# The fourth row tile of the last layer: its accumulated sums turned by DMA transposes and laid into its PSUM bank by ScalarE

## The chip, the cores and the metric

The kernel runs on one core of one Trainium2 chip. The metric is the device time of one execution in microseconds (us). Engines are named as in the profile: PE (TensorE, the matrix engine), DVE (VectorE), ACT (ScalarE), POOL (GpSimd) and SP (SyncE, which issues most DMAs). PSUM is the memory that PE writes: 8 banks of 512 float32 columns on 128 partitions. SBUF is the on-chip memory that the other engines and the DMAs use.

## The reference

Six layers of a cross network over 4096 rows of 416 features, all in bfloat16:

```
B, F, D, L = 4096, 26, 16, 6          # Din = 26 * 16 = 416
x = x0
for l in range(6):
    x = x0 * (x @ ws[l] + bs[l]) + x
return x
```

## The kernel before

By induction every layer's result is x0 times a running sum: x after layer l is x0 * (1 + the sum over all layers so far of (x @ w + b)). So the kernel never restarts its PSUM accumulation: the banks hold the running sum S, each layer adds its product, and the next x is x0 * (S + a bias column). It works on the transposed matrix (features on partitions, rows along the columns).

The 4096 rows are cut into four blocks (`s` = 0 to 3) of 1024 rows, and a block into two halves (`h`) of 512. The 416 features are three chunks (`c`) of 128 and a tail of 32. `bank(h, c)` is 3h + c: banks 0 to 2 hold half 0, banks 3 to 5 half 1; banks 6 and 7 (`T_BANK`) hold the 32 tail features of both halves.

`Plan.add` records every operation with the data that it reads and writes, and works out its semaphore waits. Each engine then runs its own list strictly in the order written. Two engines never touch one bank at once: a reader of a bank also waits for the earlier readers of it on other engines (lines 39 and 40).

One layer of one block is, on PE: `main` for half 0 (36 matmuls), `tail_rows` (what the tail adds to the six banks, in two operations), `tail_outs` (the tail's own sums), `main` for half 1. DVE's `leave` (line 435) makes the next x from a bank, one per bank. ACT's `tail_halves` (line 445) takes the tail banks, POOL multiplies them by x0 (line 458), and ACT and POOL copy the swapped pieces (lines 422, 424).

After layer 5 the results of blocks 0 to 2 stand transposed. `transpose_block` turns them with DMA transposes on SP's queue (lines 475 and 480, SBUF to SBUF), and `store_block` lays the 32 tail features beside them (POOL, line 486) and stores the block (SP, line 492). The store of block s - 1 is issued in block s at layer 3, that of block 2 thus in the last block.

The last block's layer 5 is done otherwise (from line 605), so that no transposed result is left at the end. For each of eight row tiles `j` of 128 rows, x is the stationary operand and the weights stream, so the product comes out with rows on partitions:

- `row_main(j, start, narrow)`: three products (k = 0, 1, 2) into bank `ROW_BANKS[j]`. Narrow means that each is cut into four matmuls of 32 columns of the array.
- `row_sums(j, narrow)`: the running sum S up to layer 4 has to be added, and it stands transposed. Three matmuls of `sS_sb` against an identity matrix (again times four if narrow) turn it and add it to the bank in one step.
- `row_tails()`: what the tail features add, for all eight tiles at once.
- `finish(j, ...)`: times x0, by DVE (line 665), or by ACT (line 672) and POOL (line 676); then six stores (line 683).

The running sums are saved beforehand, in the step that the code calls `ending` (block 3, layer 4): `keep_sum(h, c, engine)` copies bank(h, c), with the bias column added, to `sS_sb` (ACT, line 467, five times; DVE, line 469, once). POOL makes `st_sb`, the same for the tail (lines 579 and 584). The order in the `ending` step is: on PE all of layer 4; on DVE six `leave` and one `keep_sum`; on ACT first the two `tail_halves`, then five `keep_sum` in the order (0,0), (0,1), (0,2), (1,0), (1,1). Of the last layer PE's order is:

```
for j in range(4):
    row_main(j, True, True)
for j in range(4):
    row_sums(j, True)
row_tails()
...
for j in range(4, 8):
    row_main(j, False, False)
    row_sums(j, False)
    finish(j, None)
```

All matmuls of the program carry line 287, that of a helper, so they are told apart by their tiles: `ps<-w_sb,xT_sb` is `row_main`, `ps<-ident,sS_sb` is `row_sums`, `ps<-wt_sb,xt_sb` and `ps<-ident,st_sb` are `row_tails`.

Of the kernel before, what the change touches and what calls it, by code (L numbers as in the profile page):

```python
# [8 lines left out]
ACTF = mybir.ActivationFunctionType  # L9
# [109 lines left out]
def bass_standalone__dcn_v2_cross__recsys_kernel(  # L119
# [6 lines left out]
    B, D = x0.shape  # L126
    L = ws.shape[0]
    NC = 3
    DF = 128 * NC
# [3 lines left out]
    NS = B // SB  # L133
    H = SB // 2
# [5 lines left out]
    CH = range(NC)  # L140

    with ExitStack() as es:

        def sb(name, shape, dt=BF16):
            return es.enter_context(nc.sbuf_tensor(name, shape, dt))
# [12 lines left out]
        t32_sb = sb("t32_sb", [128, 2, G], FP32)  # L158
        sS_sb = sb("sS_sb", [128, NC, SB])
        st_sb = sb("st_sb", [128, G])  # L160
        f32_sb = sb("f32_sb", [128, 2, D], FP32)
        xo_sb = sb("xo_sb", [128, NS - 1, NC, SB])
        xot_sb = sb("xot_sb", [128, NS - 1, G])
# [9 lines left out]
        ps = es.enter_context(nc.psum_tensor("ps", [128, 8, 512], FP32))  # L173
# [5 lines left out]
        P = Plan()  # L179
# [51 lines left out]
        for k in CH:  # L231
# [19 lines left out]
            writes=[("dummy",)],  # L251
# [12 lines left out]
                out=u_sb[:, :], in_=ones_sb[:, 0:L], pattern=[[1, L]],  # L264
                compare_op=ALU.is_ge, fill=0.0, base=1, channel_multiplier=-1,
            ), reads=[("ones",)], writes=[("u",)],
        )
        P.add("gpsimd", lambda e: e.memset(wc_sb[:, :, :], 0.0), writes=[("wc", "wt%d" % i) for i in range(3)])

        def replicate():  # L270
            for g, eng in ((1, "gpsimd"), (3, "scalar"), (2, "gpsimd")):
# [156 lines left out]
        def leave(s, l, h, c):  # L428
            if l == L - 1:
                dst, key = xo_sb[:, s, c, h * H:(h + 1) * H], ("xo", s, c, h)  # L430
            else:
                dst, key = xT_sb[:, (l + 1) % 2, c, h * H:(h + 1) * H], ("xT", (l + 1) % 2, c, h)
            o = s * SB + h * H
            P.add(
                "vector", lambda e: e.scalar_tensor_tensor(  # L435
                    out=dst, in0=ps[:, bank(h, c), :], scalar=cb_sb[:, c, l:l + 1], in1=x0T_sb[:, c, o:o + H],
                    op0=ALU.add, op1=ALU.mult,
                ), reads=[("ps", bank(h, c)), ("cb",), ("x0T", s, c, h)], writes=[key],
            )
# [24 lines left out]
        def keep_sum(h, c, eng):  # L464
            o, i, b = sS_sb[:, c, h * H:(h + 1) * H], ps[:, bank(h, c), :], cb_sb[:, c, L - 1:L]
            if eng == "scalar":
                fn = lambda e: e.activation(out=o, in_=i, func=ACTF.Identity, bias=b)  # L467
            else:
                fn = lambda e: e.tensor_scalar_add(o, i, b)
            P.add(eng, fn, reads=[("ps", bank(h, c)), ("cb",)], writes=[("sS", c, h)])  # L470

        def transpose_block(s):
            for c in CH:
                P.add(
                    "sync", lambda e, c=c: e.dma_start_transpose(
                        o_sb[:, s * JS:(s + 1) * JS, c * 128:(c + 1) * 128], xo_sb[:, s, c, :]
                    ), reads=[("xo", s, c, h) for h in HALVES], writes=[("o", s)], dma="oT%d" % s,
                )
            P.add(
                "sync", lambda e: e.dma_start_transpose(ot_sb[:, s, :, :], xot_sb[:, s, :]),  # L480
                reads=[("xot", s)], writes=[("ot", s)], dma="ot%d" % s,
            )
# [60 lines left out]
        for s in range(NS):  # L543
            for l in range(L):
                ending = s == NS - 1 and l == L - 2
                if s == NS - 1 and l == L - 1:
                    break
                if s == 0 and l == 0:
                    for k in CH:
                        for part in range(2) if k == 0 else (None,):  # L550
                            for m in CH:
                                main(s, l, 0, m, k, part)
                        if k == 1:
                            tail_in()
                            bias_sums()
                    tail_rows(s, l, True)
                    for c in CH:
                        leave(s, l, 0, c)
                    tail_outs(s, l, False)
                else:  # L560
                    for m in CH:
                        for k in CH:
                            main(s, l, 0, m, k)
                    tail_rows(s, l, l == 0)
                    for c in CH:
                        leave(s, l, 0, c)
                    tail_outs(s, l, False)
                if s == 0 and l == 1:
                    corner(2, L, "wt2")
                leave_tail(s, l, not ending)  # L570
                if l == 2 and 0 < s < NS - 1:
                    place_tail(s + 1)
                if s == 0 and l == 0:
                    corner(1, 2, "wt1")
                if l == 3 and s > 0:
                    store_block(s - 1)
                if ending:
                    P.add(
                        "gpsimd", lambda e: e.tensor_tensor(
                            out=bt_sb[:, :], in0=cb_sb[:, NC, L - 1:L], in1=cb_sb[:, NC, L - 2:L - 1], op=ALU.subtract  # L580
                        ), reads=[("cb",)], writes=[("bt",)],
                    )
                    P.add(
                        "gpsimd", lambda e, t=t32_sb[:, l % 2, :]: e.tensor_scalar_add(st_sb[:, :], t, bt_sb[:, :]),
                        reads=[("t32", l % 2), ("bt",)], writes=[("st",)],
                    )
                    for c in CH:
                        keep_sum(0, c, "scalar")
                for m in CH:
                    for k in CH:  # L590
                        main(s, l, 1, m, k)
                    leave(s, l, 1, m)
                if ending:
                    for c in CH:
                        keep_sum(1, c, ("scalar", "scalar", "vector")[c])
            if s < NS - 1:
                transpose_block(s)
            if s < NS - 2:
                load_transposed(s + 2, 0, SB)
                load_last_columns(s + 2)  # L600
            if s == NS - 2:
                load("sync", xr_sb[:, :, :], x0_v[:, (NS - 1) * JS:NJ, :], "xr", [("xr",)])


        s, l = NS - 1, L - 1
        ROW_BANKS = (6, 7, 0, 1, 2, 3, 4, 5)
        src, off = src_main(s, l)
        srct, tkey = src_tail(s, l)

# [7 lines left out]
        def row_main(j, start, narrow):  # L617
            b, h = ROW_BANKS[j], j // 4
            for k in CH:
                P.add(  # L620
                    "tensor", lambda pe, k=k: row_mm(
                        pe, ps[:, b, 0:D], src[:, k, off + j * 128:off + (j + 1) * 128], w_sb[:, l, k, :],
                        start and k == 0, narrow,
                    ), reads=[("w", l), src_key(s, l, k, h)], adds=[("ps", b)],
                )

        def row_sums(j, narrow):
            b, h = ROW_BANKS[j], j // 4

            def fn(pe):  # L630
                for c in CH:
                    ins = row_mm(
                        pe, ps[:, b, c * 128:(c + 1) * 128], sS_sb[:, c, j * 128:(j + 1) * 128], ident[:, :], False, narrow
                    )
                return ins

            P.add("tensor", fn, reads=[("ident",)] + [("sS", c, h) for c in CH], adds=[("ps", b)])

        def row_tails():
            for r in range(2):  # L640
                def fn(pe, r=r):
                    for g in range(4):
                        b = ROW_BANKS[2 * g + r]
                        mm(
                            pe, ps[:, b, 0:D], srct[quad(g), 0, r * 128:(r + 1) * 128], wt_sb[quad(g), l, :],
                            g >= 2, (32 * g, 0),
                        )
                    for g in range(4):
                        b = ROW_BANKS[2 * g + r]
                        ins = mm(  # L650
                            pe, ps[:, b, DF:D], st_sb[quad(g), r * 128:(r + 1) * 128], ident[quad(g), quad(g)],
                            False, (32 * g, 0),
                        )
                    return ins

                P.add(
                    "tensor", fn, reads=[("wt", wkey(l)), tkey, ("st",), ("ident",)],
                    adds=[("ps", ROW_BANKS[2 * g + r]) for g in range(4)],
                )
# [24 lines left out]
                reads=[("ol", j) for j in range(a, b)], writes=[("outl", a)], dma="outl%d" % a,  # L684
            )

        for j in range(4):
            row_main(j, True, True)
        for j in range(4):
            row_sums(j, True)  # L690
        row_tails()
        finish(0, None)
        finish(1, 0)
# [40 lines left out]
```

## Time and profile before

| what | value |
|---|---|
| runs | 128.41, 128.68, 128.70 us; median 128.68 us |
| the profiled execution | 128.06 us, of which its span (first to last instruction) is 126.6 us |
| PE busy | 123.0 us, 97% of the span, 2414 matmuls |
| DVE busy | 99.6 us, 79% |
| ACT busy | 43.6 us, 34% |
| POOL busy | 38.8 us, 31% |
| last layer of the last block | PE from 117.56 us to the end of its matmuls at about 123.9 us |
| last store | issued at 124.56 us, the last landing near the end of the span |
| store of block 2 | issued at 114.06 us; the three block stores take 4.4 us (median) from issue to landing |

The span is counted from the first instruction; all times below are from there. A group's duration is that of one instruction, but matmuls overlap in the array: 48 matmuls of 339 ns each are done in 2.28 us, so what a matmul costs PE is the distance to the next one. The chain of waits is the sequence of work that ended last, followed back from the end. "From issue to landing" of a DMA counts from the start of its issue on the queue's engine until its semaphore says that the data is there.

### The profile page before, as it was taken

What the parts mean: (1) busy time and instruction counts of PE and PEld (TensorE: products, weight loads), DVE (VectorE), ACT (ScalarE), POOL (GpSimd) and SP (SyncE); (2) the same over time, 40 slices, a digit from 0 to 9 for tenths busy, and PEclk for the clock granted to TensorE, in tenths of its full rate; (3) what the DMA queues carried; (4) which work ended last, traced back from release to release, by engine and by line L of the source; (5) the groups of instructions that cost most, each with busy time, mean ns of one, the idle gap of its engine ahead of it and who ended that gap; (6) DMA issues with size and microseconds to landing.
All of it is one profiled execution on the core that took longest, in us unless ns stands there. A gap on an engine that the chain in (4) does not pass through costs nothing.

```text
span 126.6 us, 5307 instructions
## 1 busy us (share of the span) xinstructions
PE 123.0 (97%) x2414; PEld 64.3 (51%) x2414; DVE 99.6 (79%) x156; ACT 43.6 (34%) x95; POOL 38.8 (31%) x81
## 2 busy tenths in 40 slices
PE   7999999999999999999999999999999999999991
PEld 5554554554555554545545545545545545555660
DVE  2467978879879779779779789788797797797873
ACT  2342523424205225225205224233223252253820
POOL 6505404314204124144014043152122241350450
PEclk9999999999999999999999999999999999999999
DMA  3998998100059791016037893108009480006117
GB/s 99 237 240 226 292 199 107 28 19 0 8 114 161 167 166 28 22 54 226 0 86 169 68 218 87 31 5 269 5 9 203 80 257 0 5 0 226 49 39 236
DMA packets 34934, 14.03 MB, mean 111 GB/s; under 512 B 25722, under 2 KB 34912, under 8 KB 34912
## 3 DMA queue, kind: packets, MB, share of 16 engines
q1 hardware_dynamic: 33744, 13.20, 47.3%
q10 hardware_dynamic: 1136, 0.49, 1.4%
q8 instruction: 19, 0.31, 1.0%
q14 instruction: 3, 0.02, 0.1%
q0 software_dynamic: 32, 0.01, 0.0%
HBM read 3.79 MB, written 3.41 MB: 57 GB/s over the span
## 4 chain that ended last, share of the span: by engine, by line
PE 97%; DVE 0%; issue 0%
PE ps L287 94%; PE ps L295 2%; PE ps L506 1%; DVE o_sb L665 0%
## 5 line engine op out<-in xcount | busy, mean ns | idle before, releaser
L435 DVE SCALAR_TENSOR_TENSOR xT_sb<-ps,cb_sb,x0T_sb 128x512 bf16<-128x512 f32 x120 | 80.9, 743 | 16.5 <-PE ps L287 16.5
L287 PE MATMUL ps<-xT_sb,w_sb 128*32 128x512 bf16 (+1 forms) x1596 | 84.2, 364 | 0.0
L287 PEld LDWEIGHTS ps<-xT_sb,w_sb 128*32 128x32 bf16 x1596 | 40.9, 97 | 37.2 <-issue 4.0
L445 ACT ACTIVATE t_sb<-ps,cb_sb 64x256 f32<-64x256 f32 x46 | 21.6, 469 | 57.2 <-PE ps L287 56.9
L458 POOL TENSOR_TENSOR xt_sb<-t_sb,x0t_sb 128x256 bf16<-128x256 f32 x20 | 13.4, 671 | 65.2 <-ACT t_sb L445 65.2
L422 ACT ACTIVATE xt_sb<-xt_sb 32x256 bf16<-32x256 bf16 x38 | 15.7, 414 | 15.1 <-POOL xt_sb L458 14.9
L287 PE MATMUL ps<-x0T_sb,w_sb 128*32 128x512 bf16 (+1 forms) x348 | 18.6, 358 | 0.1
L424 POOL COPY xt_sb<-xt_sb 32x256 bf16<-32x256 bf16 x38 | 14.9, 392 | 2.4
L435 DVE SCALAR_TENSOR_TENSOR xo_sb<-ps,cb_sb,x0T_sb 128x512 bf16<-128x512 f32 x18 | 12.1, 743 | 2.5 <-PE ps L287 2.5
L287 PEld LDWEIGHTS ps<-x0T_sb,w_sb 128*32 128x32 bf16 x348 | 8.8, 96 | 7.5 <-issue 0.8
L287 PE MATMUL ps<-xt_sb,wt_sb 32*128 32x512 bf16 (+1 forms) x152 | 11.6, 326 | 0.0
L287 PE MATMUL ps<-xt_sb,wc_sb 32*128 32x256 bf16 x76 | 7.3, 268 | 0.0
L287 PEld LDWEIGHTS ps<-xt_sb,wt_sb 32*128 32x128 bf16 x152 | 2.3, 91 | 8.1 <-DVE xT_sb L435 8.1
L458 POOL TENSOR_TENSOR xot_sb<-t_sb,x0t_sb 128x256 bf16<-128x256 f32 x3 | 2.0, 671 | 9.9 <-ACT t_sb L445 9.9
L287 PE MATMUL ps<-w_sb,xT_sb 128*32 128x416 bf16 (+1 forms) x60 | 5.1, 339 | 0.0
L665 DVE TENSOR_TENSOR o_sb<-ps,xr_sb 128x416 bf16<-128x416 f32 x6 | 3.4, 587 | 1.3 <-PE ps L287 1.0
L287 PEld LDWEIGHTS ps<-xt_sb,wc_sb 32*128 32x128 bf16 x76 | 3.9, 93 | 0.2
L295 PE MATMUL ps<-const-bfloat16-1.0 128*128 128x256 bf16 x14 | 3.1, 414 | 0.8 <-PEq L719 0.8
L516 DVE COPY x0T_sb<-ps 128x256 bf16<-128x256 bf16 x6 | 1.3, 282 | 2.4 <-PE ps L506 2.4
L467 ACT ACTIVATE sS_sb<-ps,cb_sb 128x512 bf16<-128x512 f32 x5 | 3.0, 691 | 0.0
L287 PEld LDWEIGHTS ps<-w_sb,xT_sb 128*32 128x32 bf16 (+1 forms) x60 | 2.3, 97 | 1.4 <-issue 0.2
L676 POOL TENSOR_TENSOR o_sb<-f_sb,xr_sb 128x416 bf16<-128x416 f32 x2 | 1.9, 978 | 2.9 <-ACT f_sb L672 2.9
(43 smaller groups left out, 28.2 us busy)
## 6 DMA issues: line engine op xcount, KB each, us to landing
out_dram<-o_sb SPq DMA_DIRECT2D x3, 832.0 KB, 4.4
w_sb<-in_ws_dram SPq DMA_DIRECT2D x5, 312.0 KB, 3.9
xr_sb<-in_x_dram SPq DMA_DIRECT2D x1, 832.0 KB, 5.1
wt_sb<-in_ws_dram SPq DMA_DIRECT2D x4, 104.0 KB, 3.2
out_dram<-o_sb SPq DMA_DIRECT2D x2, 208.0 KB, 2.2
w_sb<-in_ws_dram SPq DMA_DIRECT2D x3, 104.0 KB, 3.7
xin_sb<-in_x_dram ACTq DMA_DIRECT2D x1, 208.0 KB, 3.4
xin_sb<-in_x_dram SPq DMA_DIRECT2D x1, 208.0 KB, 3.1
```

The lines of the kernel that those rows point to most:

```text
L287: return pe.matmul(dst, lhsT=lhsT, rhs=rhs, start=start, stop=True, skip_group_check=True, tile_position=pos,)
L295: ins = pe.matmul(ps[:, 7, 0:256], lhsT=const[:, 0:128], rhs=const, start=True, stop=True)
L422: fn = lambda e, d=dst, s=src: e.activation(out=d, in_=s, func=ACTF.Copy)
L424: fn = lambda e, d=dst, s=src: e.tensor_copy(out=d, in_=s)
L435: "vector", lambda e: e.scalar_tensor_tensor(out=dst, in0=ps[:, bank(h, c), :], scalar=cb_sb[:, c, l:l + 1], in1=x0T_sb[:, c, o:o + H], op ...
L445: "scalar", lambda e, p=p, h=h: e.activation(out=dst[p, :], in_=ps[p, T_BANK[h], 0:G], func=ACTF.Identity, bias=cb_sb[p, NC, l:l + 1]), re ...
L458: "gpsimd", lambda e: e.tensor_tensor(out=dst, in0=t, in1=x0t_sb[:, s, 0, :], op=ALU.mult),
L467: fn = lambda e: e.activation(out=o, in_=i, func=ACTF.Identity, bias=b)
L506: ins = pe.transpose(out=psT[:, b, j * 128:(j + 1) * 128], in_=xin_sb[:, 2 * i + j, c * 128:(c + 1) * 128], identity=ident[:, :],)
L516: "vector", lambda e, d=dst, s=src: e.tensor_copy(out=d, in_=s),
L665: "vector", lambda e: e.tensor_tensor(out=o_sb[:, jj, :], in0=ps[:, b, 0:D], in1=xr_sb[:, j, :], op=ALU.mult), reads=[("ps", b), ("xr",)], ...
L676: "gpsimd", lambda e: e.tensor_tensor(out=o_sb[:, jj, :], in0=t, in1=xr_sb[:, j, :], op=ALU.mult),
```

## The change

The fourth row tile (j = 3, `LAID`) no longer gets its running sum by PE's `row_sums`. Instead:

- SP issues three DMA transposes of 128 by 128 (`transpose_sums`), one for each feature chunk in the order c = 2, 0, 1, from `sS_sb` into a new tile `sr_sb`, which then holds the sum with rows on partitions.
- ACT copies `sr_sb` (128 by 416) into the tile's PSUM bank. The 32 columns of the tail are zeros, set once by POOL early in the kernel.
- PE's `row_main(3)` then adds its product to what stands in the bank (start is False), and so comes after the sums of tiles 0 to 2.

So that the three sums are there early, the three `keep_sum` of half 0 come before the two `tail_halves` on ACT, in the order c = 2, 0, 1, and the third is read by ACT before DVE's `leave` reads that bank. The banks of the row tiles are dealt out otherwise (tiles 0 to 4 use banks 0, 1, 6, 2, 7). The store of block 2 is issued at layer 2 of the last block instead of layer 3.

```diff
+        sr_sb = sb("sr_sb", [128, D])
...
+        P.add("gpsimd", lambda e: e.memset(sr_sb[:, DF:D], 0.0), writes=[("srz",)])
...
+        def transpose_sums(col):
+            for c in (2, 0, 1):
+                P.add(
+                    "sync", lambda e, c=c: e.dma_start_transpose(
+                        sr_sb[:, c * 128:(c + 1) * 128], sS_sb[:, c, col:col + 128]
+                    ), reads=[("sS", c, 0)], writes=[("sr",)], dma="sr",
+                )
...
-                    for c in CH:
-                        leave(s, l, 0, c)
+                    if ending:
+                        leave(s, l, 0, 0)
+                        keep_sum(0, 2, "scalar")
+                        keep_sum(0, 0, "scalar")
+                        leave(s, l, 0, 1)
+                        leave(s, l, 0, 2)
+                        keep_sum(0, 1, "scalar")
+                        transpose_sums(H - 128)
+                    else:
+                        for c in CH:
+                            leave(s, l, 0, c)
                     tail_outs(s, l, False)
...
-                if l == 3 and s > 0:
+                if s > 0 and l == (3 if s < NS - 1 else 2):
                     store_block(s - 1)
...
-                    for c in CH:
-                        keep_sum(0, c, "scalar")
...
-        ROW_BANKS = (6, 7, 0, 1, 2, 3, 4, 5)
+        ROW_BANKS = (0, 1, 6, 2, 7, 3, 4, 5)
+        LAID = 3
...
-        for j in range(4):
+        for j in range(LAID):
             row_main(j, True, True)
-        for j in range(4):
+        for j in range(LAID):
             row_sums(j, True)
+        P.add(
+            "scalar", lambda e: e.activation(out=ps[:, ROW_BANKS[LAID], 0:D], in_=sr_sb[:, :], func=ACTF.Copy),
+            reads=[("sr",), ("srz",)], writes=[("ps", ROW_BANKS[LAID])],
+        )
+        row_main(LAID, False, True)
         row_tails()
```

## The prediction

> **What bounds the kernel now.** I read first the chain of waits on the page, to see which engine a saved instruction helps:
>
> ```profile
> PE 97%; DVE 0%; issue 0%
> PE ps L287 94%; PE ps L295 2%; PE ps L506 1%; DVE o_sb L665 0%
> ```
>
> It is PE from end to end: a matmul less shortens the span, and any pause of PE lengthens it by as much. So I read PE's rows of the last 12 us in the timeline (columns: start, us from the first start to the last end, engine, line, operation, tiles, shape, count):
>
> ```profile
> 114.97 0.38 PE L287 MATMUL ps<-xt_sb,wc_sb 32*128 32x256 bf16 x3
> ...
> 117.56 2.28 PE L287 MATMUL ps<-w_sb,xT_sb 128*32 128x416 bf16 x48
> 119.67 0.84 PE L287 MATMUL ps<-ident,sS_sb 128*32 128x128 bf16 x48
> 120.44 0.35 PE L287 MATMUL ps<-wt_sb,xt_sb 32*128 32x416 bf16 x4
> ```
>
> The reader sees no gap: the four narrow row tiles start at 117.56, their sums at 119.67, the tails at 120.44. Tile j = 3 is a quarter of the first two rows. Then the same stretch on the engines that the change reorders:
>
> ```profile
> 115.19 4.04 DVE L435 SCALAR_TENSOR_TENSOR xT_sb<-ps,cb_sb,x0T_sb 128x512 bf16<-128x512 f32 x6 [0.84 <-PE ps L287]
> 115.84 0.96 ACT L445 ACTIVATE t_sb<-ps,cb_sb 64x256 f32<-64x256 f32 x2 [2.30 <-PE ps L287]
> 116.83 3.00 ACT L467 ACTIVATE sS_sb<-ps,cb_sb 128x512 bf16<-128x512 f32 x5
> 117.81 0.93 POOL L584 TENSOR_SCALAR st_sb<-t_sb,bt_sb 128x256 bf16<-128x256 f32 x1
> ```
>
> A kept sum takes 0.69 us and the next starts 0.57 after it; a `leave` takes 0.74 and the next starts 0.66 after it. Last, what a DMA transpose from SBUF to SBUF costs: SP's timeline in a stretch without other traffic, then the answers by tile for o_sb and for ot_sb (durations of the issue in ns, min/median/max; then issue to landing in us):
>
> ```profile
> 64.28 4.01 SPq L475 DMA_TRANSPOSE o_sb<-xo_sb  x3
> 68.33 1.24 SPq L480 DMA_TRANSPOSE ot_sb<-xot_sb  x1
> ```
>
> ```profile
> L475 SPq DMA_TRANSPOSE o_sb<-xo_sb x9: 1244/1307/1311, 35.0 to 96.2; - x9
> ...
> DMA to landing us min/median/max: 1.8/2.8/4.5
> ```
>
> ```profile
> L480 SPq DMA_TRANSPOSE ot_sb<-xot_sb x3: 1244/1596/1768, 39.0 to 97.6; - x3
> ...
> DMA to landing us min/median/max: 2.4/2.8/2.9
> ```
>
> The reader is to see that the issue does not shrink with the size: 128x1024 takes SP 1.24 to 1.31 us, 128x256 no less than 1.24. SP issues one after the other.
>
> **What it removes.** Twelve of the 48 narrow matmuls against the identity. The 48 cost PE 120.44 - 119.67 = 0.776 us, so the gain is 0.194 us. Even alone that is 0.15% of 128.68; a measurement of this kernel tells about 0.3%, or 0.39 us, from no change.
>
> **What it adds: a chain that ends in PE's list.** `row_main(3)` now waits for ACT's copy, the copy for three transposes, these for three kept sums. Step by step, with 0.05 us for each hand-over (PE's last `tail_outs` ends at 115.79, ACT starts at 115.84; ACT's second tail copy ends at 116.80, POOL starts at 116.88):
>
> - Kept sum of c = 2: bank 2 is complete when the wc_sb matmuls end, 114.97 + 0.38 = 115.35. ACT 115.40 to 116.09.
> - c = 0: waits for the first `leave`, 115.19 + 0.75 = 115.94. ACT 115.99 to 116.68.
> - c = 1: waits for the second `leave`, 115.86 + 0.74 = 116.60. ACT 116.65 to 117.34.
> - Transposes: the first is issued at 116.14. I take 1.244 us of issue for each (the 128x256 row is the nearest) and 0.045 between issues: the second starts at 117.43, the third at 118.72, each after its sum is there. Data would be ready at 117.4, but SP is still busy with the two before it.
> - The third lands 2.42 us after its issue started (the undisturbed ot_sb transpose at 68.33): 121.14.
> - ACT's copy of 128x416, priced by the f_sb<-ps copies of that shape (513 to 517 ns): 121.19 to 121.71. `row_main(3)` can start at 121.76.
>
> Without the wait PE would be there at 117.56 + 3 x 0.528 (2.11 / 4 each) + 3 x 0.194 = 119.72. The stall is 2.04 us; less the 0.194 that is saved, everything from `row_tails` on comes 1.85 us later. Half the columns move in half the time (256 columns' data take roughly 0.3 us of the landing), which takes off some 0.1: I take **+1.8 us**. Nothing makes it up: after the stall come `row_main(3)`, the tails, four wide tiles, the last `finish` and store, each behind the other, as before.
>
> Bounds of the unknown price of a 128x128 transpose. From below, the shortest SBUF-to-SBUF DMAs that are no transposes (the x0t_sb pieces: issue 0.52, landing 1.75); the landing then is 117.39 + 1.75 = 119.14, but ACT reaches its copy only after the two tail copies and the kept sums (1,0) and (1,1), at about 119.45, so PE starts at 120.0: stall 0.3, net **+0.1**. That floor holds for free transposes too. From above, the slowest rows: issue 1.31, landing 4.5: 116.14 + 2 x 1.355 + 4.5 = 123.35, PE at 123.97, net **+4.1**. I stay by the 128x256 row.
>
> The Trainium skill speaks against the change ("VectorE: DVE Perf Modes", § Rules for kernel authors): a 128x128 transpose belongs on TensorE where the result may go to PSUM, and on the DMA crossbar otherwise. Its § The three transpose paths gives 1309 ns for the DMA; this trace has such a price for the issue alone.
>
> **What is moved, at no cost.** In each case the cover is named.
>
> - The two tail copies go behind three kept sums: 117.25 to 118.2 instead of 115.84 to 116.80, 1.4 us later. POOL's chain behind them (0.67, 0.19, 0.93) ends at about 120.15 instead of 118.74. `row_tails` needs it; before it started at 120.44, now not before 120.25 even without a stall. Margin 0.1, covered by the stall; gone, it would cost at most 0.1.
> - The third `leave` waits for the kept sum of c = 2 (116.09); DVE reaches it at 116.52. Margin 0.4.
> - `row_main(0)`, (1), (2) wait for ACT's reads of banks 0, 1, 6: 116.68, 117.34, about 117.7, against PE's 117.56, 118.08, 118.61. Margins 0.9, 0.7, 0.9.
> - Queued behind ACT's waiting copy: only the two `finish` copies, which need `row_tails` anyway. Behind SP's transposes: the last stores, over 3 us later.
> - Block 2's store and its POOL copy: POOL is free from 108.7 (after layer 2's swaps) until 112.0, the copy takes 0.4. The store lands about 4.4 us after 109.2, so its traffic is gone before the transposes.
> - The memset of 128x32: the memset of 128x1344 ends at 3.72, POOL then waits about 1.0 us for weights.
>
> **The rivals.**
>
> - *Short issue, nothing to measure* (the other side). If an issue scaled with size, or cost what a plain DMA's costs (0.52), the chain would be hidden up to ACT's order: +0.1, 128.8. For it: 128x128 occurs in no row. Against it: a quarter of the columns saved 5% of the issue. It decides below about 0.75 us an issue (landing 1.18 us after the issue's end, as at 68.33). Faster by 0.39 us is not in it, since PE saves 0.194 in all.
> - *One price for the whole transpose.* If one is over, landing included, when its 1.31 us end, the data is there at 116.14 + 3 x 1.31 = 120.07, PE at 120.69, net +0.8: 129.5. Against it: every transpose row lands 1.2 us or more after its issue ended. (The skill's 1309 ns, read as the whole time, would give this.)
> - *Late landing.* Behind the first transpose of the batches at 35 and 94 us the others landed after 2.8 to 4.5 us, in the batch at 64 us after 2.4 to 2.8. If something holds up the last one here, so that it takes 2.9 to 4.5, the net is +2.3 to +4.1: 131 to 132.8. For it: two of three batches. Against it: these three move an eighth of the data, with the queue nearly empty.
> - *PE runs slow after its pause.* The first 14 matmuls of 256 columns start 0.22 us apart, later ones of that width 0.11: PE starts the program at half pace. If a stall of 2 us brought that back, the 4.0 us from `row_main(3)` on would take up to 8: +5.8, 134.5. The trace has no pause over 0.11 us in PE after its first matmul, so it can't say. The Trainium skill ("TensorE: Matmul & The Clock Gate", § HAM oscillation) warns of idle gaps over about 3.4 us. By that rule a stall of 2 us leaves the clock alone, and only the worst late landing would not; I give it little.
>
> **How the numbers follow.** Forecast 0.72; late landing 0.11; one price 0.05; slow PE 0.03; short issue 0.09, of which I give 0.02 to something unseen that makes it faster. The profiled execution would go from 128.06 to 129.9. It lay 0.62 under the median of the runs shown, 128.68; against that the forecast is **130.5 us**. The forecast's own range is 130.0 to 131.0 (+1.3 to +2.3: issue 1.1 to 1.3, landing 2.2 to 2.6). With the one-price case and the nearer half of the late landings the range is 129.3 to 131.8. Faster 0.02, same 0.07, slower 0.91.
>
> **What would show it.** Right: on PE a gap of about 2 us before the last 12 matmuls ps<-w_sb,xT_sb of the narrow kind, ended by ACT; three sr_sb<-sS_sb issues of about 1.24 us back to back from 116.1; ACT's copy near 121.2; the rows before 117.56 unmoved. Wrong: issues under 0.75 us, or a gap under 0.5 us; a gap at another place (`row_tails` waiting for POOL, row tile 0 for ACT); matmuls of the wide tiles further apart than before.

## The result, and the profile after

| | before | after |
|---|---|---|
| median of 6 runs each | 128.59 us | 129.94 us (129.20 to 130.66) |
| ratio, 95% interval | 1 | 1.0115 (1.0085 to 1.0145), that is +1.1 to +1.9 us |
| the profiled execution, its span | 128.06, 126.6 us | 130.07, 128.6 us |

The changed kernel is slower. In its code the same operations stand some lines lower: the matmul helper is line 289, `keep_sum` 469, `tail_halves` 447, ACT's copy into PSUM 710, the new transposes 477. The chain of waits of the changed kernel has links that it did not have:

```profile
PE 92%; ACT 3%; DMA 2%; DVE 0%; SPq 0%; issue 0%
PE ps L289 89%; PE ps L297 2%; DMA sr_sb<-sS_sb 2%; ACT sS_sb L469 1%; PE ps L516 1%; ACT t_sb L447 1%; DVE o_sb L683 0%; ACT ps L710 0%; SPq L477 0%
```

In order of time, an excerpt (start, length, what):

```profile
118.81 0.04 issue
118.85 2.33 DMA sr_sb<-sS_sb
121.18 0.02 issue
121.20 0.53 ACT ps L710
121.73 0.04 issue
121.78 4.12 PE ps L289 x52
```

The last transpose, the copy, then PE: nothing else is between them. PE's timeline of the changed kernel:

```profile
117.67 1.76 PE L289 MATMUL ps<-w_sb,xT_sb 128*32 128x416 bf16 x36
119.25 0.68 PE L289 MATMUL ps<-ident,sS_sb 128*32 128x128 bf16 x36
121.78 0.71 PE L289 MATMUL ps<-w_sb,xT_sb 128*32 128x416 bf16 x12 [1.84 <-ACT ps L710]
122.42 0.35 PE L289 MATMUL ps<-wt_sb,xt_sb 32*128 32x416 bf16 x4
```

36 matmuls of the sums instead of 48, and then 1.84 us of idle PE, ended by ACT's copy (the last line is `row_tails`). SP and ACT in the same stretch, from their timelines:

```profile
109.30 0.38 SPq L502 DMA_DIRECT2D out_dram<-o_sb  x1
116.23 3.85 SPq L477 DMA_TRANSPOSE sr_sb<-sS_sb  x3
```

```profile
115.52 1.92 ACT L469 ACTIVATE sS_sb<-ps,cb_sb 128x512 bf16<-128x512 f32 x3 [1.87 <-PE ps L289]
117.33 0.95 ACT L447 ACTIVATE t_sb<-ps,cb_sb 64x256 f32<-64x256 f32 x2
118.31 1.26 ACT L469 ACTIVATE sS_sb<-ps,cb_sb 128x512 bf16<-128x512 f32 x2
121.20 0.52 ACT L710 ACTIVATE ps<-sr_sb 128x416 f32<-128x416 bf16 x1 [1.63 <-DMA sr_sb<-sS_sb]
```

The three sums are ready at 117.44 (115.52 + 1.92). SP's three issues last until 120.08, and ACT is idle for 1.63 us before its copy.

One measure serves for all runs below: the **end stretch**, from the first `ps<-w_sb,xT_sb` matmul (row tile 0) to the issue of the last store. It was 124.56 - 117.56 = 7.00 us before and is 126.53 - 117.67 = 8.86 after. What lies ahead of it moved by 0.11 us here, and in the profiles of this study row tile 0 began between 117.35 and 118.32, whatever the kernel; the landings of the first loads differ from run to run. So the end stretch shows tenths of a us where a median of runs does not.

### The profile page after: what moved, and what is told of

Its sections match the earlier page's. It is cut to its first block, busy times and chain, and to the rows that moved or that the text cites. A ratio compares the mean times of both kernels' runs of the same rounds, so it can differ in the third digit from the quotient of the medians.

```text
span 128.6 us, 5287 instructions
## 1 busy us (share of the span) xinstructions
PE 123.2 (96%) x2402; PEld 64.6 (50%) x2402; DVE 99.7 (78%) x156; ACT 44.2 (34%) x96; POOL 38.8 (30%) x82
## 3 DMA queue, kind: packets, MB, share of 16 engines
HBM read 3.79 MB, written 3.41 MB: 56 GB/s over the span
## 4 chain that ended last, share of the span: by engine, by line
PE 92%; ACT 3%; DMA 2%; DVE 0%; SPq 0%; issue 0%
PE ps L289 89%; PE ps L297 2%; DMA sr_sb<-sS_sb 2%; ACT sS_sb L469 1%; PE ps L516 1%; ACT t_sb L447 1%; DVE o_sb L683 0%; ACT ps L710 0%; SPq L477 0%
```

## The experiments

The edits are shortened: `...` stands for lines left out, and words in brackets or behind "as" describe code. Each is made in the changed kernel unless another is named. A median is followed by that of the kernel before, measured in the same set, and by the ratio of the two with its 95% interval.

**The changed kernel again** (no edit).

> The changed kernel once more, unaltered, for a second profile and more runs. The theory (three issues of about 1.23 us one after the other on SP, a landing of 2.33, a copy of 0.52, and PE waiting for it): PE stands 1.8 to 2.0 us before row_main(3), and its first row tile and last store lie as far apart as in the first profile; the time is 1.3 to 1.9 us over the kernel before. A rival, that the stall varies with other DMA traffic: a stall that differs by over 0.3 us from the 1.84 of the first profile.

Median 129.85 against 128.49, ratio 1.0106 (1.0073 to 1.0140). End stretch 8.68 us (117.35 to 126.03), PE idle for 1.67 us, a little under the 1.8 to 2.0 that was expected. SP's timeline of this run shows the 0.17 us that are missing to 1.84:

```profile
115.91 3.68 SPq L477 DMA_TRANSPOSE sr_sb<-sS_sb  x3
```

3.68 instead of 3.85: the first issue took 1.13 instead of 1.30 us, the other two 1.23 in both. The stall follows the issues.

**The moved parts alone.**

```diff
-        LAID = 3
+        LAID = 4
-        (the ACT copy, row_main(LAID, False, True), transpose_sums, the memset)
```

> What the change moves without what it adds: the order of the last copies, the banks of the row tiles and the earlier store of block 2 stay, but the fourth tile's sums are turned by PE as before, and there are no transposes, no copy into PSUM and no memset. The theory (the moved parts are hidden): within 0.15 us of the kernel before; row_tails, which waits for POOL's st_sb, starts at most 0.1 us late. The rival (the moved parts cost a good part of the loss): at least 0.5 us slower.

128.54 against 128.49, ratio 1.0006 (0.9981 to 1.0030), end stretch 7.00 us. PE's timeline of it:

```profile
118.10 2.28 PE L288 MATMUL ps<-w_sb,xT_sb 128*32 128x416 bf16 x48
...
120.99 0.35 PE L288 MATMUL ps<-wt_sb,xt_sb 32*128 32x416 bf16 x4
```

From the first row to the tails 2.89 us, against 2.88 before: the copies' new order, the banks and the earlier store cost nothing that can be measured.

**The transposes, with nobody waiting.** As the last one, with the memset and the three transposes back; only the end of the kernel waits for them.

> As e1_order_only, but the three transposes and the memset are there, and nothing but the end of the kernel waits for them: PE turns the fourth tile's sums, there is no copy into PSUM. The theory (the wait costs, not the transposes themselves): within 0.2 us of the kernel before, three issues of 1.23 to 1.30 us on SP. The rival (the transposes slow other engines or delay the last stores): at least 0.5 us slower.

128.09 against 128.49, ratio 0.9977 (0.9955 to 0.9999), end stretch 7.00 us with SP issuing from 116.88 for 3.68 us. The transposes disturb nothing; the wait for them does. That the runs came out 0.3 us faster has no counterpart in the end stretch.

**The memset alone, in the kernel before.** This is to see whether the memset makes that 0.3 us.

> The kernel before with the memset of 128x32 on POOL early on, and nothing else (the tile is never read). Every kernel of this study that has this memset came out 0.1 to 0.5 us below what its last 12 us in the profile say; e1_order_only, which lacks it, did not. The theory (the memset is hidden, and the difference is the scatter of the first loads, whose landings move the whole span by up to 1 us from run to run): within 0.2 us of the kernel before. The rival (the memset speeds up the first microseconds): 0.2 to 0.5 us faster.

128.16 against 128.41, ratio 0.9993 (0.9971 to 1.0015), end stretch 7.00 us. The memset is no gain that the interval tells from nothing. Most kernels with transposes came out up to 0.4 us faster in the runs than their end stretch says; the one with the wider transposes and the one with the late store (both below) came out 0.1 us slower. The cause stays open; scatter of the first loads could explain it, but that was not shown.

**One transpose for three.** The kept sums are laid out tile by tile, so the fourth tile's are one block of 384 columns.

```diff
-        sS_sb = sb("sS_sb", [128, NC, SB])
+        sS_sb = sb("sS_sb", [128, JS, NC, 128])
...
-            for c in (2, 0, 1):
-                ... dma_start_transpose(sr_sb[:, c * 128:(c + 1) * 128], sS_sb[:, c, col:col + 128])
+            dma_start_transpose(sr_sb[:, 0:DF] as (c f), sS_sb[:, 3, :, :] as 384 columns)
```

> The changed kernel with the kept sums laid out tile by tile, so that one transpose of 128x384 takes the place of three of 128x128. It is issued when the last of the three sums is there, at about 117.5 us. The theory (an issue costs about 1.25 us whatever its size): landing at about 119.95, copy until 120.5, PE waits about 0.75 instead of 1.84; 0.4 to 0.8 us slower than the kernel before, 1.1 to 1.3 faster than the changed kernel. The rival (the issue costs by size, about 0.42 us for each 128 columns, or more by blocks): an issue of about 3 us or more, and no faster than the changed kernel.

128.73 against 128.49, ratio 1.0017 (0.9993 to 1.0041); end stretch 7.44 us, 1.2 to 1.4 less than with three. SP's and PE's timelines:

```profile
117.27 1.20 SPq L476 DMA_TRANSPOSE sr_sb<-sS_sb  x1
```

```profile
120.17 0.71 PE L289 MATMUL ps<-w_sb,xT_sb 128*32 128x416 bf16 x12 [0.43 <-ACT ps L709]
```

Three times the columns in one issue of 1.20 us, starting later, and still PE waits 0.43 instead of 1.84. The price is by the issue, not by the size. The expectation had the wait at 0.75 and the loss at 0.4 to 0.8 us; the runs show a loss of 0.2, which their interval does not tell from nothing, the end stretch 0.44.

**Three transposes of four times the size.**

```diff
-                        sr_sb[:, c * 128:(c + 1) * 128], sS_sb[:, c, col:col + 128]
+                        sr_sb[:, :, c * 128:(c + 1) * 128], sS_sb[:, c, 0:H]      # sr_sb is [128, 4, D]
```

> The changed kernel with three transposes of 128x512 (all four row tiles of the half) instead of 128x128; only the fourth tile's part is used. The theory (an issue of fixed cost, data at some 290 GB/s): issues of 1.25 to 1.31 us, a landing 0.1 to 0.3 us later, 0.1 to 0.5 us slower than the changed kernel. The rival (the price goes by size): four times the issue, a stall of 8 us or more.

130.18 (4 runs) against 128.35, ratio 1.0156 (1.0105 to 1.0207). The answer by tile for sr_sb (issue in ns, min/median/max; landing in us):

```profile
L477 SPq DMA_TRANSPOSE sr_sb<-sS_sb x3: 1205/1265/1275, 116.1 to 118.7; - x3
...
DMA to landing us min/median/max: 2.3/2.4/2.4
```

An issue of 128x512 takes 1.27 us where 128x128 took 1.23, and the last lands after 2.38 instead of 2.33, so 0.05 us later where 0.1 to 0.3 was expected. End stretch 8.87 us, as with the small ones.

**Two, and one.** PE adds the chunks that are not turned (four narrow matmuls each); the memset covers the whole tile, so ACT lays zeros in their columns.

```diff
-            for c in (2, 0, 1):
+            for c in (2, 0):                 # e6: (2,)
...
         row_main(LAID, False, True)
+        row_sums(LAID, True, (1,))           # e6: (0, 1)
```

> The changed kernel with two transposes (chunks 2 and 0); the columns of chunk 1 are zero in the tile that ACT lays, and PE adds that chunk's sum of the fourth tile with four narrow matmuls. The theory: one issue less on SP, so the data lands at about 119.9, 1.27 us earlier than with three; the copy ends at about 120.5, PE waits about 0.7 us; 0.5 to 0.8 us slower than the kernel before. The rival (the landing or the copy sets the wait, not the number of issues): a wait within 0.3 us of the 1.84 with three.

> As e5_two with the transpose of chunk 2 alone; PE adds chunks 0 and 1 of the fourth tile. It lands at about 118.6. The theory: ACT, which does its list in order, comes to the copy only after the kept sums (1,0) and (1,1), at about 119.6, so the copy ends at about 120.1 and PE waits about 0.3 us although the data was there 1 us earlier; 0.2 to 0.45 us slower than the kernel before. The rival (the landing alone sets the wait): no wait, and no slower than the kernel before.

Two: 129.08 against 128.35, ratio 1.0040 (1.0020 to 1.0059), end stretch 7.68 us, PE idle for 0.61. One: 128.57, ratio 1.0007 (0.9984 to 1.0030), end stretch 7.24. With one the times alone decide nothing; its timeline on ACT does:

```profile
118.42 1.27 ACT L469 ACTIVATE sS_sb<-ps,cb_sb 128x512 bf16<-128x512 f32 x2
119.57 0.52 ACT L710 ACTIVATE ps<-sr_sb 128x416 f32<-128x416 bf16 x1
```

The transpose was issued at 116.34 and landed 2.5 us later, at 118.84, but ACT was at the kept sums (1,0) and (1,1). The copy has no idle time ahead of it: the order of ACT's list sets it. By an estimate from the trace, PE could have been there 2.09 us after row tile 0: 1.58 for the 36 matmuls of `row_main`, and 9 x 0.056 for the sums of three tiles, whose groups of four start 0.056 us apart. (This takes the step from the sums to `row_main(3)` as free, as the step from `row_main` to the sums is.) That is 119.87, and `row_main(3)` started at 120.15, 0.28 us later. From one to two transposes the end stretch grows by 0.44, from two to three by 1.0 to 1.2; an issue is hidden only until that place in ACT's list.

PE's timeline of the same run also prices the sums:

```profile
120.15 0.71 PE L289 MATMUL ps<-w_sb,xT_sb 128*32 128x416 bf16 x12
120.69 0.28 PE L289 MATMUL ps<-ident,sS_sb 128*32 128x128 bf16 x8
120.90 0.35 PE L289 MATMUL ps<-wt_sb,xt_sb 32*128 32x416 bf16 x4
```

Two chunks of sums take 0.21 us until the tails start; the one chunk of the kernel with two transposes takes 0.16 (121.22 to 121.38). So a chunk costs about 0.05, and 0.1 belongs to the passage from narrow matmuls (128*32 in the rows) to those of the tails (32*128). `row_main(3)` takes 0.54 us until the sums start, where a narrow row takes 0.53 in a stream without a wait; in the changed kernel, where the tails come next, it takes 0.64 (121.78 to 122.42).

**Work beside the wait.** As with one transpose, and PE does the fifth tile first.

```diff
+        row_main(4, True, False)
+        row_sums(4, False)
         row_main(LAID, False, True)
...
-                            g >= 2, (32 * g, 0),
+                            g >= 2 and 2 * g + r != 4, (32 * g, 0),
```

> As e3_one_issue (one transpose), and PE does the fifth row tile's product and sums (0.70 us) before the fourth tile's, so the wait has work beside it; row_tails then adds to the fifth tile instead of starting it. The theory (what PE waits for comes at about 120.6): no wait over 0.15 us is left, and PE's matmuls end some 0.1 us earlier than before; but DVE gets tiles 0, 2 and 4 at once after row_tails and ends no earlier: within 0.25 us of the kernel before. The rival (the wait moves behind): 0.5 us slower or more.

128.84 against 128.35, ratio 1.0029 (1.0009 to 1.0049), end stretch 7.41 us. PE's wait is gone, but the loss is above the 0.25 us that the expectation allowed. DVE's and SP's timelines:

```profile
121.53 3.08 DVE L682 TENSOR_TENSOR o_sb<-ps,xr_sb 128x416 bf16<-128x416 f32 x6 [1.74 <-PE ps L289]
```

```profile
123.38 1.94 SPq L700 DMA_DIRECT2D out_dram<-o_sb  x4
```

Six `finish` in 3.08 us without a gap; before they took 3.65 us and waited for PE in between. They start 0.76 us later after row tile 0 (4.08 instead of 3.32), since `row_tails` comes later, and end 0.19 later. The other 0.22 us are SP's: its four store issues follow each other without a pause, and the last starts at 124.86, 0.25 us after the last `finish`; before it started 0.03 after it. PE gained nothing either: its last matmul starts 6.18 us after row tile 0, against 6.12 before. PE's timeline shows why:

```profile
119.64 0.70 PE L289 MATMUL ps<-w_sb,xT_sb 128*128 128x416 bf16 x3
...
120.44 0.71 PE L289 MATMUL ps<-w_sb,xT_sb 128*32 128x416 bf16 x12
121.09 0.35 PE L289 MATMUL ps<-wt_sb,xt_sb 32*128 32x416 bf16 x4
```

Two passages are new, from narrow to wide matmuls (128*128) and back: in the trace the wide row starts 0.16 us after the last group of narrow sums, and `row_main(3)` 0.15 after the last wide sum, where sums in a row start 0.056 apart. These 0.2 us eat up what the turned tile saves. And `row_main(3)` takes 0.65 us until the tails although PE did not wait before it, so the 0.64 of the changed kernel is not a price of its wait.

**The store where it was.** The changed kernel with block 2's store at layer 3.

```diff
-                if s > 0 and l == (3 if s < NS - 1 else 2):
+                if s > 0 and l == 3:
```

> The changed kernel with the store of block 2 back at layer 3 of the last block (issued at about 114.1 us, landing at about 118.5 to 119.8, so its data is in flight when the first transpose is). The theory: it can hold up the first transposes, but the third has its data moved only at about 120.1, after the store has landed: PE's wait stays within 0.3 us of the 1.84 of the changed kernel and the time within 0.4 us of it. The rival (the store's traffic reaches the last transpose): a wait longer by 0.5 us or more.

130.82 against 128.41, ratio 1.0192 (1.0167 to 1.0216), where the changed kernel has 1.0106 to 1.0115; end stretch 9.36 us, PE idle for 2.35. The answer by tile for sr_sb:

```profile
L477 SPq DMA_TRANSPOSE sr_sb<-sS_sb x3: 1127/1234/1887, 116.4 to 119.5; - x3
...
DMA to landing us min/median/max: 2.3/3.0/3.9
```

PE's wait was expected within 0.3 us of 1.84 and came out 0.51 longer. I expected the third transpose to be untouched, and its own issue (1.234) and landing (2.34) are. But the first landed after 3.9 us, beside the store's data (the store itself landed at 120.01), and the second's issue was drawn out to 1.89 us, so the third started 0.65 us late. So the early store belongs to the change, and is worth about 0.5 to 0.7 us in the end stretch.

**Six transposes.** The three sums go first into a tile that is not read, then into the right one. This kernel ran once.

```diff
-            for c in (2, 0, 1):
+            for c, dst in ((2, sd_sb), (0, sd_sb), (1, sd_sb), (2, sr_sb), (0, sr_sb), (1, sr_sb)):
```

> The changed kernel with six transposes on SP: the three sums are first turned into a tile that nobody reads, then into the right one. The theory: three issues more, 3 x 1.27 = 3.8 us, so PE waits about 5.6 us. This also shows what a long pause does to PE: the theory of the prediction gives slow matmuls no place after a pause of 2 us; if a pause of 5.6 us brings back the pace of the first microseconds, the wide row tiles (0.70 us each) take up to twice as long, and the time is up to 3.5 us above the 133.7 that the wait alone gives; if not, they still take 0.70 us.

137.22 us, the upper end of what was expected for a PE that resumes at half pace. SP's six issues take 3.81 and 3.79 us, PE idles for 5.64 us. PE's timeline, then the busy times by stretch (each engine's busy us and instructions; PEclk is the granted clock, with 1.00 for full speed):

```profile
125.86 1.23 PE L290 MATMUL ps<-w_sb,xT_sb 128*32 128x416 bf16 x12 [5.64 <-ACT ps L711]
...
130.58 1.25 PE L290 MATMUL ps<-w_sb,xT_sb 128*128 128x416 bf16 x3
...
131.94 0.71 PE L290 MATMUL ps<-w_sb,xT_sb 128*128 128x416 bf16 x3
```

```profile
core 0: us, PE busy (x) PEld busy (x) DVE busy (x) ACT busy (x) POOL busy (x), PEclk, DMA share, GB/s
119.90:124.00 4.10, 0.32 (x24) 0.14 (x12) 0.40 (x1) 0.00 (x0) 0.61 (x1) 1.00 0.11 24
124.00:125.50 1.50, 0.00 (x0) 0.00 (x0) 0.00 (x0) 0.22 (x1) 0.00 (x0) 0.88 0.10 22
125.50:129.00 3.50, 3.14 (x32) 1.14 (x33) 1.09 (x2) 1.23 (x3) 0.39 (x1) 0.50 0.02 5
```

The granted clock falls while PE waits, after 124.0, and is 0.50 when PE resumes; wide tiles start 1.33 to 1.36 us apart instead of 0.70 until about 131.9. In the changed kernel, with 1.84 us of idle time, they stay at 0.70 (122.92, 123.63, 124.32, 125.02). This is as the Trainium skill has it ("TensorE: Matmul & The Clock Gate", § HAM oscillation): idle gaps over about 3.4 us cost the clock. Here 2.35 us did not (the kernel with the late store, granted clock 1.00), 5.64 did; where between them the limit lies no run here shows.

## Why the prediction was right, point by point

Times of the changed kernel are given as seen; its row tile 0 starts 0.11 us later than before.

- **The bound.** PE from end to end: shown. From row tile 0 to the tails PE took 2.88 us before (117.56 to 120.44) and takes 4.75 now (117.67 to 122.42); from the tails to the last store's issue it is 4.1 us in both. So the whole growth of 1.86 us lies ahead of the tails, and it is one stall less one saving: PE could have begun `row_main(3)` at 117.67 + 2.09 = 119.76 and began at 121.78, which is 2.02 us; 0.17 is saved. (The 1.84 of idle time counts from the modelled end of the last matmul, 119.94.)
- **The gain.** 0.194 was a quarter of 0.776 us, but not all of the 0.776 is sums. In the trace of the kernel before, the last group of four sums starts 0.162 us ahead of the tails, and the others 0.056 apart; the difference of 0.106 is the passage to the tails, which the changed kernel pays too, behind `row_main(3)`. Twelve sums cost 3 x 0.056 = 0.17 us. The direction is the same, the prize is smaller still.
- **The chain.** Kept sums from 115.40 to 117.34: measured 115.52 to 117.44. Third issue at 118.72: 118.85. Landing 2.42: 2.33. Copy ends at 121.71: 121.72. Stall 2.04: 2.02. Each within 0.1 us when the 0.11 is taken off; in the stall two errors cancel, since the copy ended 0.10 us earlier than forecast and PE could have been there 0.08 earlier.
- **Half the columns in half the time.** The prediction took 0.1 us off for this, at 0.3 us for 256 columns' data. The landing did come out 0.09 shorter than that of 128x256, but no run shows this reason: 128x512 landed after 2.38 us where 128x128 took 2.33, so 384 columns more cost 0.05. That this term fitted was luck.
- **An issue of 1.24 us whatever the size.** The step on which most hung, taken from one 128x256 row: 1.230 for the second and third of 128x128, 1.20 for 128x384, 1.27 for 128x512. The one that begins a batch varies more, 1.13 to 1.40.
- **The floor by ACT's list** (+0.1 at least, even with free transposes): with one transpose, landed early, PE still starts `row_main(3)` 0.28 us late, where a stall of 0.3 was forecast. The end stretch grows by 0.24 and not by 0.1 because two of the three chunks of sums stay with PE, so that only 0.056 is saved.
- **Moved at no cost.** Shown by the kernel with the moved parts alone. Of the single covers only the store's was tried: without the early store, 0.5 to 0.7 us more. POOL's `st_sb` ended at 120.22, against about 120.38 when `row_tails` would have come without the wait: the margin was real, 0.16 us. Block 2's store landed 5.66 us after its issue, not 4.4, at 114.96; that is still ahead of the first transpose.
- **The rivals.** Short issue: refuted (1.23). One price for the whole transpose: refuted, landing 2.33. (In the kernel before, the transpose at 97.56 landed 1.14 us after its issue's end, so "1.2 us or more" was a little high; nothing hangs on it.) Late landing: didn't occur in the two profiles of the changed kernel, and the late store shows one way to it. Slow PE: not at 1.84 us, but it is real at 5.64.
- **The size in the runs.** 130.5 was forecast, 129.94 measured: inside the range of 129.3 to 131.8, and 0.06 us below the forecast's own 130.0 to 131.0. The stall's size was right in the profile. Of the 0.56, about 0.1 to 0.2 is the base: 128.68 was taken, the kernel before has 128.49 and 128.59 in the larger sets. The rest: the spans of the changed kernel's twelve runs are 1.5 to 1.6 us over those before on average, where the profiles' end stretch gives 1.7 to 1.9, and what lies outside the span is 1.38 us on average instead of 1.53. The cause of both is open.

No version here that takes sums off PE beats the kernel before. What the change can save is 0.17 us, 0.13%, which these runs cannot tell from nothing, and each way to shorten the wait or fill it left a larger bill in the end stretch: 0.44 us with one transpose, 0.24 with one chunk, 0.41 with work put beside it.

## What to carry to other kernels

Before work is moved from the bounding engine to a queue, the whole chain to the data's return has to be set against the time until the bounding engine needs it: here 0.17 us of matmuls were exchanged for three issues in a row, a landing and a copy, 4.3 us from the last kept sum. The small DMA transposes here cost by their number, so it pays to lay the data out for one of them. Filling a wait with other work of the same engine helps only if the engines behind it, here DVE, POOL and SP, do not get their work later for it. And before a group's duration is divided by its count, its last member has to be looked at: the passage to the next kind of work may be in it.

## What the runs showed of the hardware that was not expected

- The issue of a DMA transpose from SBUF to SBUF costs SP about the same for 128x128 (1.23 us) and 128x512 (1.27 us).
- With a plain store in flight, two things changed for the transposes issued behind it: the first landed after 3.92 us instead of 2.40, and the next one's issue took SP 1.89 us instead of 1.23.
- Where PE goes from matmuls of one shape in the array to another (128*32, 128*128 and 32*128 in the rows) it loses about 0.1 us, at a granted clock of 1.00. The tails start 0.16 us after the last group of narrow sums instead of 0.056 (kernel before). They start 0.28 after the last group of `row_main(3)` instead of 0.176, in the changed kernel and just so in the kernel with work beside the wait, where PE had not waited. Narrow to wide and back costs 0.1 each time. The reason was not tested.
